# Folding the even frequencies of the first transform a third time, with part of the fold on GpSimd

## The chip, the cores and the metric

The kernel runs on one core of one Trainium2 chip. The metric is the device time of one execution in microseconds. A core has five engines that run side by side, each through its own instructions in a fixed order, and wait for one another through semaphores: PE (TensorE) multiplies matrices, DVE (VectorE) and ACT (ScalarE) work element by element, POOL (GpSimd) does so too and issues transfers, SP (SyncE) here only issues transfers. PEld is PE's loading of weights, which runs beside its matmuls.

## The reference

```python
def _attn_ref(x):                       # x: (8, 1856, 256) float32
    X = np.fft.fft(x, axis=1)
    X = np.fft.fft(X, axis=2)
    return X.real.astype(np.float32)

def _moe_ref(x, w_group, w_expert, w1, w2):   # x: (14848, 256)
    g_idx = np.argmax(x @ w_group, axis=1)    # 4 groups; g_w = its softmax weight
    ...
    for g in range(4):
        e_idx = np.argmax(x[g_idx == g] @ w_expert[g], axis=1)   # 4 experts per group; e_w
        for e in range(4):
            h = np.maximum(xg[mask_e] @ w1[g, e], 0.0)           # 256 -> 1024
            ye = h @ w2[g, e]                                    # 1024 -> 256
            out[tok_idx] = combined[:, None] * ye                # combined = g_w * e_w
```

The real part of a two-dimensional Fourier transform of each of 8 batches of 1856 x 256 gives 14848 tokens; each goes to one of 16 experts (256 to 1024 to 256), and the result is scaled by the two softmax weights.

## The kernel before

**The first transform.** It runs over the 1856 positions of a batch, as matrix multiplication with cosine and sine tables (`CS`, resident in on-chip memory). Symmetry cuts the work before that. The host lays out x in four quarters (`_layout`): positions s, 928 - s, -s and 928 + s, for s = 0 to 464, in 4 chunks of 128 rows, the mirrored two with their columns reversed. `fold` (one generator per batch) adds these quarters: `fold_rows` adds the two halves of x on DVE for batches 0 and 1; for later batches the second half is added by the transfer itself (`load_x`: one plain load on SP's queue, then two accumulating loads that POOL issues). `squares` and `total` give the sum of squares for a power-of-two scale. `quarters(pm)` adds (pm = 0) or subtracts (pm = 1) the remaining two halves, two DVE instructions of 128x514 each, from `xa` into `xc` (both tiles named `xq`). `columns(eo, ...)` folds the 256 columns (eo = 0 adds, 1 subtracts) into `BD[:, pm, eo]`, 512 columns wide: 4 chunks of 128. `hi_half` (ACT) scales to float16 as the high half of `ghl`, `lo_half` (DVE) makes the rest, the low half.

`s_stage` multiplies: for odd frequencies (par = 1, 464 of them) and even ones (par = 0, 465), and for cosine (tr = 0) and sine (tr = 1, 127 weight columns), 12 matmuls add up in a bank `pu`: 4 chunks of positions times three products of high and low halves. `sums` lists them. For par = 1 the products with the high half come first. Then the sum is split into float16 halves `U` (`split_later`: ACT copies it, PE subtracts it, ACT copies the rest). The same sums for the Nyquist column of all batches run once, with 8 weight columns (`xngh`, `nyquist_in`, `nyquist`); their result goes through memory (`UND`, `UN`, then row 127 of `U` for each batch, scaled in `un`).

**After it.** `d_stage` is the second transform, over features, of the batch before (`pr`, with the router's logits into `look`); `route` finds the experts and each token's place (DVE mostly), `leftovers` lets POOL copy odd tiles into `Um`, `lookup` turns places into gather indices (`ii_e`). The expert stage (`phase2`, lines 1296 to 1317: `ph`, `py`) gathers rows with indirect transfers (`xg`), transposes them (`xT`) and begins while the last batch is still being routed.

**What sets the order.** All steps of the first stage are generators, and the tables `START` and `ORDER0` to `ORDER8` at the top of the file are the order in which they are advanced, one letter a step: S is `s_stage`, D `d_stage`, R `route`, T and Z `lookup` and the rest of an older route, F and N the folds of the next and the next but one batch, L, U, W, X leftovers, Nyquist rows, first weights and first gathered rows; G and H the fold of batch 0 and the Nyquist preparation; small letters release queued copies (l: low halves, s, I, i: splits, d: rows). Each engine then keeps the order in which instructions were written (`InOrder`), so a step that waits holds back all that stands behind it on its engine. The line 281 in the profile is the call in `InOrder` through which all of these are recorded, so tiles tell them apart.

Buffers: `xq` has four halves, two per batch, so batch b + 2 is loaded into those of batch b; `BD` has one buffer, `ghl` two, `pu` four banks, `pr` two.

Of the kernel before, what the change touches and what calls it, by code (L numbers as in the profile page):

```python
# [57 lines left out]
START = 'iTGHDiHFGGGtHGI'  # L58
ORDER0 = 'WSDDGYZSlZZZFFWRiSdSDFdIDLilFisiFZsTItFFldtUIdLRSiFtilFilSdI'
ORDER1 = 'ZZsLDbldDsDDlDIIdDdRSFblLDFSULdStFiFFFlRIRRFStRiRSRRRtNRUZDRNRURbTlITLdRtNTNSRNslsTUILIFsStTRtTsSRTRiSTSSI'  # L60
ORDER2 = 'ldslZZFZUDZLLRDtlIDDddSZDTFRiZlsssRsDbIZbLsSSFDLRiiRFSsDRRlRNTRURtISdRDTNRNTIdRRtdSFRdsSZNTFiTTbNtRTRUSUsTSSSIN'
ORDER3 = 'IZDslILiFZDIlLZLdFUZZRTFlUDSFdSSLFSLSSDItFTFRRDSIFURLDRRsRTDFRNRTSSFLsiRTDISITTURRsSNRNRUNTITRRRNR'
ORDER4 = 'bstZTDDDZdDbLIDlDLULDFlDSLslZDItiDRbdFRRSUDlIZFFTstSisDLIRNSSINDUsRdNINtsRbFiTRRISRDTSSNRRTTRDiTTlRU'
ORDER5 = 'DUslITSIFdFbLRIIZSRDLRdsZSZlIbZNIFRSsZRFDSsdRRSdUDlINLRRDUsLlTNRFlDRSIsssdtSTNFUITNFUlbRiUZdTUDRTsZT'
ORDER6 = 'DTSSFLdstRtsIFtZZlIRLdSZRZsILIUUIRZNLFRNSSLRNLDdLRUDLRZlNDbNNTiNsSFtLsLlDLITSTDsTNdNNisRUlLsTFiZRdNR'
ORDER7 = 'IZNWSSZZtLNLdFdiFDLFiDsFdWUDTdZZZSUDDdlsdtlDdLIRDRRdRRDWRWtRSRSSsiXUiRINRRLtZslTRDSXIIiWXlRbTStRXXRtsUWXWiXlTtXLSWWUllSRbRXWIWWWTTXbilWSWWWTWbWWWWTsW'
ORDER8 = 'IDsiDdDLdRbLLddDRdLsLRiDdRDR|RDDLLbidbTsiRTRRRRRTRLdisbLRRld|R|RRRRDRLRRLRRRR'
# [5 lines left out]
CW = 4 * NK  # L73
# [229 lines left out]
class K:  # L303
# [82 lines left out]
    def nyquist_in(self):  # L386
# [29 lines left out]
        V.tensor_tensor(out=gv, in0=gv, in1=bc(sn[:, :], 1, 8), op=ALU.mult)  # L416
        yield
# [59 lines left out]
    def fold(self, b, x, fp):  # L477
# [58 lines left out]
        if b == 0:  # L536
# [4 lines left out]
            quarters(0)  # L541
            columns(0, 0, 1)
# [406 lines left out]
    def phase1(self):  # L949
# [4 lines left out]
        with tc.tile_pool(name="ua", bufs=1) as ua, tc.tile_pool(name="fft", bufs=1) as fp:  # L954
# [616 lines left out]
```

## Time and profile before

| what | value |
|---|---|
| time, median of 3 runs | 895.41 us (891.83 to 895.62) |
| the profiled execution | 892.05 us, span 890.2 us |
| PE busy | 823.2 us, 92% (6491 matmuls) |
| DVE / ACT / POOL busy | 546.6 / 577.0 / 313.5 us |
| first matmul of the expert stage | at 193.5 us |
| first transform's matmuls | 384, with 83.8 us busy |

The span runs from the first to the last instruction. A busy PE is not PE at its peak: matmuls follow each other before the former has ended, so the spacing of their starts says more than their length. The same holds for DVE, whose instructions overlap by some 0.08 us. An engine's share over the whole span mixes stages; the rows below are therefore mostly of stretches.

### The profile page before, as it was taken

The page shows a single profiled execution, that of the slowest core. Times are in us where ns is not written, and L with a number is a line of the kernel's source. Part 1 is how long each engine was busy: PE and PEld are TensorE (multiplying, and loading weights), DVE is VectorE, ACT ScalarE, POOL GpSimd, SP SyncE. Part 2 cuts the span into 40 slices and gives each one's busy share as a digit, 9 for nine tenths or more (in the row PEclk, how much of TensorE's full clock was granted, in tenths as well). Part 3 has the DMA queues.
Part 4 walks back from the last instruction along what each step waited for, and adds up shares of the span by engine and source line. Part 5 has one row for each costly group of instructions (what it writes and reads, how often), then busy time and mean ns, then how long its engine had stood idle before and what let it go on. Part 6 is the DMA issues. An engine that isn't in the chain of part 4 may idle for free.

```text
span 890.2 us, 17777 instructions
## 1 busy us (share of the span) xinstructions
PE 823.2 (92%) x6491; PEld 587.2 (66%) x6491; DVE 546.6 (61%) x1381; ACT 577.0 (65%) x1190; POOL 313.5 (35%) x326
## 2 busy tenths in 40 slices
PE   2799999889697999999999999999999999999996
PEld 0367666556455767776767676767676768686865
DVE  6479998579574656464747474747474756564440
ACT  2477676576633877586858585858686777775541
POOL 1032211412674524434343434344343435240303
PEclk9999999899999999999999999999999999999999
DMA  9677863364667355555646454646555746443201
GB/s 351 176 226 201 243 210 121 137 210 138 186 180 197 111 189 181 158 155 166 173 156 178 149 166 155 173 160 172 161 176 152 196 147 206 127 137 66 55 10 41
DMA packets 105515, 144.53 MB, mean 162 GB/s; under 512 B 75194, under 2 KB 77638, under 8 KB 103888
## 3 DMA queue, kind: packets, MB, share of 16 engines
q1 hardware_dynamic: 91360, 106.15, 39.4%
q0 software_dynamic: 13632, 36.99, 14.5%
q8 instruction: 52, 0.85, 0.4%
q10 hardware_dynamic: 432, 0.22, 0.1%
q14 instruction: 39, 0.32, 0.1%
HBM read 97.41 MB, written 31.72 MB: 145 GB/s over the span
## 4 chain that ended last, share of the span: by engine, by line
PE 58%; DVE 11%; issue 8%; ACT 5%; DMA 5%; POOL 2%; another core or an unknown queue 2%; SPq 1%; POOLq 0%; DVEq 0%; ACTq 0%
PE ph L1296 29%; PE py L1312 24%; DMA xT<-xh 3%; PE pu L281 2%; ACT whl L281 2%; POOL out L940 2%; PE pr L281 1%; DVE whl L281 1%; DMA wst<-w 1%; DVE xq L281 1%; ACT junk L281 1%; SPq L1266 1%; DVE ghl L281 1%; DVE xT L281 1%
## 5 line engine op out<-in xcount | busy, mean ns | idle before, releaser
L1312 PE MATMUL py<-whl,hT 128*128 128x256 f16 x2976 | 357.4, 273 | 13.6 <-ACT y L1317 9.8
L1296 PE MATMUL ph<-xT,whl 128*128 128x512 f16 (+2 forms) x2112 | 358.4, 318 | 10.6 <-DMA xT<-xh 4.8
L1312 PEld LDWEIGHTS <-hT 128*128 128x128 f16 x2976 | 289.2, 98 | 71.4 <-issue 15.2
L1300 DVE SCALAR_TENSOR_TENSOR hT<-ph,hT 128x512 f16<-128x512 f32 (+2 forms) x352 | 179.7, 529 | 194.1 <-ACT hT L1299 126.6
L1296 PEld LDWEIGHTS <-whl 128*128 128x128 f16 x2112 | 182.5, 98 | 134.1 <-issue 16.6
L940 POOL DMA_INDIRECT out<-y,tok x124 | 147.3, 1188 | 332.2 <-ACT y L1317 266.2
L1299 ACT ACTIVATE hT<-ph 128x512 f16<-128x512 f32 (+2 forms) x352 | 157.2, 473 | 116.0 <-PE ph L1296 68.1
L281 DVE SCALAR_TENSOR_TENSOR whl<-wst,e_v,whl 128x1024 f16<-128x1024 f32 x112 | 138.0, 1279 | 20.1 <-ACT whl L281 18.0
L1238 POOL DMA_INDIRECT xg<-XS,ii_s x100 | 105.5, 1055 | 86.7 <-ACT xh L1258 35.7
L281 ACT ACTIVATE whl<-wst,e_v 128x1024 f16<-128x1024 f32 x112 | 121.0, 1138 | 15.2 <-DVE e_v L281 11.4
L281 ACT ACTIVATE junk<-wst 128x1024 bf16<-128x1024 f32 x112 | 119.2, 1064 | 6.0 <-DMA wst<-w 5.1
L1317 ACT ACTIVATE y<-py,cws 128x256 f32<-128x256 f32 x124 | 57.2, 471 | 52.0 <-PE py L1312 41.2
L281 PE MATMUL pu<-CS,ghl 128*128 128x464 f16 (+3 forms) x384 | 83.8, 370 | 3.5 <-ACT ghl L281 3.5
L1260 DVE TENSOR_TENSOR xh<-xg,xh 128x256 f16<-128x256 f32 x112 | 46.3, 418 | 48.7 <-ACT xh L1258 35.7
L1258 ACT CAST xh<-xg 128x256 f16<-128x256 f32 x112 | 42.4, 402 | 38.6 <-DMA xT<-xh 34.7
L281 PEld LDWEIGHTS <-ghl 128*128 128x128 f16 (+1 forms) x384 | 44.5, 120 | 33.2 <-issue 3.6
L281 PEld LDWEIGHTS <-U 128*128 128x128 f16 x672 | 44.9, 100 | 19.2 <-issue 7.0
L281 PE MATMUL pr<-c,U 128*128 128x256 f16 x336 | 49.9, 286 | 4.9 <-DMA U<-un 2.5
L281 ACT CAST U<-pu 128x464 f16<-128x464 f32 (+3 forms) x64 | 32.8, 548 | 20.0 <-PE pu L281 19.0
L281 POOL DMA_DIRECT2D xq<-xq x12 | 11.0, 1072 | 88.5 <-ACT xT L281 27.1
L281 DVE TENSOR_TENSOR xq<-xq 128x514 f32<-128x514 f32 x40 | 25.4, 688 | 6.4 <-DMA xq<-xq 6.2
L281 ACT ACTIVATION_READ_ACCUMULATOR junk<-wst 128x1 f32 x112 | 23.2, 207 | 0.0
(184 smaller groups left out, 461.1 us busy)
## 6 DMA issues: line engine op xcount, KB each, us to landing
wst<-w SPq DMA_DIRECT2D x108, 512.0 KB
xq<-xq SPq DMA_DIRECT2D x8, 1028.0 KB
xq<-xq POOLq DMA_DIRECT2D x12, 514.0 KB
XS<-whl SPq DMA_DIRECT2D x6, 910.0 KB
CS<-cs SPq DMA_DIRECT2D x8, 464.5 KB
XS<-row SPq DMA_DIRECT2D x3, 1040.0 KB
XS<-row SPq DMA_DIRECT2D x3, 910.0 KB
XS<-xq SPq DMA_DIRECT2D x3, 910.0 KB
```

Of the source, the lines that this page charges most:

```text
L281: return self.tc.keep_in_program_order(f(*args, **kw))
L940: ins = self.nc.gpsimd.indirect_dma_start(out=out, out_offset=bass.IndirectOffsetOnAxis(ap=ap, axis=0), in_=in_, in_offset=None, bounds_ch ...
L1238: ins = self.nc.gpsimd.indirect_dma_start(out=xg[:, :].bitcast(I32), out_offset=None, in_=self.XS[:, :], in_offset=bass.IndirectOffsetOnAx ...
L1258: A.copy(xh[:, 0], xg[:, 0:D])
L1260: lo = V.tensor_tensor(out=xh[:, 1], in0=xg[:, 0:D], in1=xh[:, 0], op=ALU.subtract)
L1266: Q.dma_start(out=xT[:, :, j * P:(j + 1) * P], in_=xh, transpose=True)
L1296: nc.tensor.matmul(ph[:, 0:n * P], lhsT=w[:, wl, o:o + P], rhs=xT[:, xl * 2 + c, :], start=i == 0, stop=i == 5)
L1299: nc.scalar.activation(hT[:, f, 0], ph[:, 0:n * P], AF.Relu)
L1300: nc.vector.scalar_tensor_tensor(out=hT[:, f, 1], in0=ph[:, 0:n * P], scalar=0.0, in1=hT[:, f, 0], op0=ALU.max, op1=ALU.subtract)
L1312: nc.tensor.matmul(py, lhsT=hT[:, f, hl, j * P:(j + 1) * P], rhs=w[:, wl, 2048 + f * D:2048 + (f + 1) * D], start=i == 0, stop=i == 23)
L1317: nc.scalar.activation(y, py, AF.Copy, scale=cw)
```

## The change

A third fold: for even frequencies position 464 - s has the same cosine as s or its negative, so that half of the positions are enough once sums and differences are formed. The table's even columns split into those that are 2 (232 of them) and 0 (233) modulo 4, each with 2 chunks of positions in place of 4; the host places the positions above 232 in the last two chunks in reverse (`_place`), the table shrinks from 4 x 929 to 4 x 464 + 2 x 465 columns per trigonometric function and half, and is loaded in 6 pieces in place of 8. On the chip the even column passes write to the scratch `tw` (which lies in `xa`), and `again` makes their sum and difference into `BD`, in two instructions. From batch 2 on, `quarters(0)` is done by GpSimd. For batch 0 the odd half is now folded first. The Nyquist preparation gets three small instructions. All order tables are new.

```diff
@@ -23,6 +23,7 @@
 P = 128
 KO, KE = 464, 465
 NK = KO + KE
+KH = 232
 NU = 936
 UJ, UN = 16, 117
 NT = 7
@@ -55,22 +56,22 @@
 
 
 
-START = 'iTGHDiHFGGGtHGI'
...
-ORDER2 = 'ldslZZFZUDZLLRDtlIDDddSZDTFRiZlsssRsDbIZbLsSSFDLRiiRFSsDRRlRNTRURtISdRDTNRNTIdRRtdSFRdsSZNTFiTTbNtRTRUSUsTSSSIN'
...
+START = 'llSZFGSHRHHGGGilHZsUGTL'
...
+ORDER2 = 'ZIZZtiFdFiDDFRUSDLZdTTDDtbZFsZLsssRSFNFLSTdSRSTLZsStNFSRRRTLIFRdDDRRTIUITiLRTsURTTSNsRTDTNRDNTRRRRsbIU'
...
 ORDERS = (ORDER0, ORDER1, ORDER2, ORDER3, ORDER4, ORDER5, ORDER6, ORDER7)
 WAIT = 4
 SUMS = 2
 BIG = 1.0e6
 RS = 2.0 ** -11
-CW = 4 * NK
+CW = 4 * KO + 2 * KE
 E23 = 2.0 ** 23
 
 
@@ -136,20 +137,26 @@
 
 
 def _kcols():
-    ev = np.arange(2, 928, 2)
-    n = NT * P - KO
-    return np.concatenate([np.arange(1, 929, 2), ev[:n], ev[n:], [0, 928]])
+    return np.concatenate([np.arange(1, 929, 2), np.arange(2, 928, 4), np.arange(4, 928, 4), [0, 928]])
+
+
+def _place(s):
+
+    return np.where(s <= KH, s, 256 + KO - s)
 
 
 def _constants():
-    s = np.arange(512)
+    s = np.arange(465)
     k = _kcols()
     ang = 2 * np.pi * ((s[:, None] * k[None, :]) % S) / S
-    ok = (s <= 464)[:, None]
-    cs = np.zeros((P, 2, 2, 4, NK), np.float16)
+    cs = np.zeros((P, 2, 2, CW), np.float16)
     for tr, fn in enumerate((np.cos, np.sin)):
-        for hl, m in enumerate(_hilo(np.where(ok, fn(ang), 0.0))):
-            cs[:, tr, hl] = m.reshape(4, P, NK).transpose(1, 0, 2)
+        for hl, m in enumerate(_hilo(fn(ang))):
+            odd, even = np.zeros((512, KO)), np.zeros((256, KE))
+            odd[_place(s)] = m[:, :KO]
+            even[:KH + 1] = m[:KH + 1, KO:]
+            cs[:, tr, hl, :4 * KO] = odd.reshape(4, P, KO).transpose(1, 0, 2).reshape(P, -1)
+            cs[:, tr, hl, 4 * KO:] = even.reshape(2, P, KE).transpose(1, 0, 2).reshape(P, -1)
 
     l = _features()
 
@@ -230,10 +237,11 @@
     xq = np.zeros((B, 4, 512, 257), x.dtype)
     for q in range(4):
         u = s[use[q]]
+        to = _place(u)
         if q < 2:
-            xq[:, q, u, :256] = x[:, idx[q, u], :]
+            xq[:, q, to, :256] = x[:, idx[q, u], :]
         else:
-            xq[:, q, u, 1:] = x[:, idx[q, u], ::-1]
+            xq[:, q, to, 1:] = x[:, idx[q, u], ::-1]
     xn = np.ascontiguousarray(
         xq[:, :, :, 128].reshape(B, 4, 4, P).transpose(3, 1, 2, 0)).reshape(P, -1)
     xq = np.ascontiguousarray(
@@ -414,6 +422,10 @@
         V.tensor_tensor(out=g[:, 1], in0=t[:, 0], in1=t[:, 1], op=ALU.subtract)
         gv = g.rearrange("p a (c b) -> p (a c) b", b=B)
         V.tensor_tensor(out=gv, in0=gv, in1=bc(sn[:, :], 1, 8), op=ALU.mult)
+        a, z = g[:, 0, 0:2 * B], g[:, 0, 2 * B:4 * B]
+        V.tensor_copy(out=t[:, 0, 0:2 * B], in_=a)
+        V.tensor_tensor(out=a, in0=a, in1=z, op=ALU.add)
+        V.tensor_tensor(out=z, in0=t[:, 0, 0:2 * B], in1=z, op=ALU.subtract)
         yield
         gh = self.fp.tile([P, 2, 2, 4, B], F16, name="xngh")
         ghv = gh.rearrange("p h a c b -> p h (a c b)")
@@ -453,8 +465,11 @@
 
     def sums(self, par, tr, terms):
 
-        k0, n = ((KO, KE), (0, KO))[par]
-        return [(0, n, c, cl, gl, c * NK + k0) for c in range(4) for (gl, cl) in terms]
+        if par:
+            return [(0, KO, c, cl, gl, c * KO) for c in range(4) for (gl, cl) in terms]
+        at = 4 * KO
+        return [(o, w, c + 2 * (i if tr else 1 - i), cl, gl, at + c * KE + o)
+                for i, (o, w) in enumerate(((0, KH), (KH, KE - KH))) for c in range(2) for (gl, cl) in terms]
 
     def load_x(self, b, xp, parts=1):
 
@@ -502,14 +517,23 @@
 
         def quarters(pm):
             for h in (0, 2):
-                V.tensor_tensor(out=xc[:, 4 * pm + h:4 * pm + h + 2], in0=xa[:, h:h + 2],
+                (self.G if b >= SUMS and pm == 0 else V).tensor_tensor(out=xc[:, 4 * pm + h:4 * pm + h + 2], in0=xa[:, h:h + 2],
                                 in1=xa[:, 4 + h:6 + h], op=(ALU.add, ALU.subtract)[pm])
 
-        def columns(eo, m0, m1):
-            t = xc[:, 4 * m0:4 * m1].rearrange("p (m c) d -> p m c d", c=4)
-            V.tensor_tensor(out=BD[:, m0:m1, eo].rearrange("p m (c d) -> p m c d", d=128),
-                            in0=t[:, :, :, eo:eo + 128], in1=t[:, :, :, 256 - eo:128 - eo:-1],
+        tw = xa.rearrange("p a d -> p (a d)")[:, 0:1024].rearrange("p (m n) -> p m n", m=2)
+
+        def columns(eo, m):
+            t = xc[:, 4 * m:4 * m + 4]
+            out = tw[:, m] if m == eo else BD[:, m, eo]
+            V.tensor_tensor(out=out.rearrange("p (c d) -> p c d", d=128),
+                            in0=t[:, :, eo:eo + 128], in1=t[:, :, 256 - eo:128 - eo:-1],
                             op=(ALU.add, ALU.subtract)[eo])
+
+        def again(m0, m1):
+            o = BD.rearrange("p m e n -> p (m e) n")[:, 3 * m0:3 * m1 - 2:3]
+            for i in range(2):
+                V.tensor_tensor(out=o[:, :, 256 * i:256 * i + 256], in0=tw[:, m0:m1, 0:256],
+                                in1=tw[:, m0:m1, 256:512], op=(ALU.add, ALU.subtract)[i])
 
         def lo_half(part):
             V.scalar_tensor_tensor(out=part(hl[:, 1]), in0=part(BD), scalar=sx, in1=part(hl[:, 0]),
@@ -538,18 +562,21 @@
             hl = fp.tile([P, 2, 2, 2, 512], F16, name="ghl", bufs=2)
             self.fds[b] = hl, v
             total()
-            quarters(0)
-            columns(0, 0, 1)
+            quarters(1)
+            columns(0, 1)
             V.tensor_scalar(out=ei, in0=pn.bitcast(I32), scalar1=24, scalar2=None,
                             op0=ALU.logical_shift_right)
             V.tensor_scalar(out=sx.bitcast(I32), in0=ei, scalar1=-E23, scalar2=199 * E23, op0=ALU.mult,
                             op1=ALU.add)
+            hi_half(lambda t: t[:, 1, 0])
+            quarters(0)
+            columns(0, 0)
+            again(0, 1)
             hi_half(lambda t: t[:, 0, 0])
-            quarters(1)
-            columns(0, 1, 2)
-            hi_half(lambda t: t[:, 1, 0])
-            yield
-            columns(1, 0, 2)
+            yield
+            columns(1, 0)
+            columns(1, 1)
+            again(1, 2)
             lo_half(lambda t: t[:, :, 0])
             yield
             hi_half(lambda t: t[:, :, 1])
@@ -569,9 +596,11 @@
         hl = fp.tile([P, 2, 2, 2, 512], F16, name="ghl", bufs=2)
         self.fds[b] = hl, v
         for eo in range(2):
-            for m in range(2):
-                columns(eo, m, m + 1)
-            yield
+            for m in (eo, 1 - eo):
+                columns(eo, m)
+            yield
+        again(0, 2)
+        yield
         exponent()
         yield
         exponents()
@@ -963,10 +992,11 @@
             self.load_small()
             xs = {0: self.load_x(0, xp, 2)}
             self.CS = fp.tile([P, 2, 2, CW], F16, name="CS")
-            cs = self.ap["cs"].rearrange("p (t h c k) -> p t h c k", t=2, h=2, c=4)
+            cs = self.ap["cs"].rearrange("p (t h k) -> p t h k", t=2, h=2)
+            cut = (0, 2 * KO, 4 * KO, CW)
             for tr in range(2):
-                for c in range(4):
-                    nc.sync.dma_start(out=self.CS[:, tr, :, c * NK:c * NK + NK], in_=cs[:, tr, :, c])
+                for a, z in zip(cut, cut[1:]):
+                    nc.sync.dma_start(out=self.CS[:, tr, :, a:z], in_=cs[:, tr, :, a:z])
                 if tr == 0:
                     nc.sync.dma_start(out=self.c16, in_=self.ap["c16"])
                     xs[1] = self.load_x(1, xp)
```

DVE at the start, from before batch 0's second fold to its first low halves; `xq` are the quarters (and, 512 wide, the scratch), `BD` the folded columns, `xng` the Nyquist column. Before:

```order
L281 TENSOR_TENSOR xq<-xq 128x514 x4
L281 TENSOR_TENSOR BD<-xq 128x512
L281 TENSOR_SCALAR x_ei<-misc 128x1
L281 TENSOR_SCALAR x_v<-x_ei 128x1
L281 TENSOR_TENSOR xq<-xq 128x514 x2
L281 TENSOR_TENSOR BD<-xq 128x512
L281 TENSOR_TENSOR BD<-xq 128x2x512
L281 SCALAR_TENSOR_TENSOR ghl<-BD,x_v,ghl 128x2x512
L281 TENSOR_TENSOR xnt<-xn 128x64
L281 TENSOR_TENSOR xng<-xnt 128x32 x2
L281 TENSOR_TENSOR xng<-xng,n_v_189 128x64
```

and now:

```order
L289 TENSOR_TENSOR xng<-xng 128x16
L289 TENSOR_TENSOR xng<-xnt,xng 128x16
L289 TENSOR_TENSOR xq<-xq 128x514 x4
L289 TENSOR_TENSOR BD<-xq 128x512
L289 TENSOR_SCALAR x_ei<-misc 128x1
L289 TENSOR_SCALAR x_v<-x_ei 128x1
L289 TENSOR_TENSOR xq<-xq 128x514 x2
L289 TENSOR_TENSOR xq<-xq 128x512
L289 TENSOR_TENSOR BD<-xq 128x256 x2
L289 TENSOR_TENSOR BD<-xq 128x512
L289 TENSOR_TENSOR xq<-xq 128x512
L289 TENSOR_TENSOR BD<-xq 128x256 x2
```

The Nyquist steps now stand ahead of the second fold (four more of them above these rows), and the low halves (`ghl`), which come next, have three column passes and four half passes ahead of them after the scale `x_v`.

POOL, from the accumulating loads of batch 3 on; the numbers tell buffers apart (now `xq_238` and `xq_391` are batches 2 and 3, `xq_644` batch 4; `U_243` is batch 0). Before:

```order
L281 DMA xq_386<-xq 128x1028 x2
L281 COPY Um_384<-U_234 128x2x33
L281 ISA
L281 TENSOR_SCALAR Um_384<-U_234 128x2x33
L281 COPY Um_384<-U_234 128x2x31
L281 TENSOR_SCALAR Um_384<-U_234,c32_78 128x2x31
L281 DMA xq_641<-xq 128x1028 x2
```

and now:

```order
L289 DMA xq_391<-xq 128x1028 x2
L289 COPY Um_381<-U_243 128x2x33
L289 ISA
L289 TENSOR_SCALAR Um_381<-U_243 128x2x33
L289 COPY Um_381<-U_243 128x2x31
L289 TENSOR_SCALAR Um_381<-U_243,c32_78 128x2x31
L289 TENSOR_TENSOR xq_239<-xq_238 128x514 x2
L289 TENSOR_TENSOR xq_392<-xq_391 128x514 x2
L289 DMA xq_644<-xq 128x1028 x2
```

The additions of batches 2 and 3 stand together between batch 0's leftovers and batch 4's accumulating loads.

DVE after batch 1's low halves; `mx`, `dd`, `m`, `oh` and `pe` are batch 0's route. Before:

```order
L281 SCALAR_TENSOR_TENSOR ghl<-BD,x_v,ghl 128x512 x4
L281 TENSOR_TENSOR xq<-xq 128x514 x4
L281 TENSOR_TENSOR BD<-xq 128x512 x2
L281 TENSOR_REDUCE mx<-lg 128x14
L281 TENSOR_TENSOR dd<-lg,mx 128x14x4
L281 SCALAR_TENSOR_TENSOR m_550<-dd,c_78 128x56
```

and now:

```order
L289 SCALAR_TENSOR_TENSOR ghl<-BD,x_v,ghl 128x512 x4
L289 TENSOR_SCALAR un<-UN,x_v 128x117
L289 TENSOR_REDUCE mx<-lg 128x14
L289 TENSOR_TENSOR dd<-lg,mx 128x14x4
L289 TENSOR_TENSOR xq<-xq 128x514 x2
L289 SCALAR_TENSOR_TENSOR m_544<-dd,c_78 128x56
```

Batch 2's quarters and first column passes stood before the route's first instruction; now two of the four quarters stand behind it and the column passes further on.

## Rows read from the trace of the kernel before

**Rows 1.** The chain that ended last: its shares of the span by engine and line
```profile
PE ph L1296 29%; PE py L1312 24%; DMA xT<-xh 3%; PE pu L281 2%; ACT whl L281 2%; POOL out L940 2%; PE pr L281 1%; DVE whl L281 1%; DMA wst<-w 1%; DVE xq L281 1%; ACT junk L281 1%; SPq L1266 1%; DVE ghl L281 1%; DVE xT L281 1%
```

**Rows 2.** Busy time by stretch; columns as the first line names them
```profile
core 0: us, PE busy (x) PEld busy (x) DVE busy (x) ACT busy (x) POOL busy (x), PEclk, DMA share, GB/s
44.00:157.50 113.50, 109.00 (x962) 77.17 (x963) 98.45 (x273) 79.31 (x178) 24.41 (x41) 0.98 0.67 197
62.00:116.40 54.40, 53.47 (x482) 37.99 (x481) 51.61 (x141) 40.76 (x91) 15.36 (x22) 1.00 0.80 235
157.50:194.00 36.50, 29.28 (x235) 19.86 (x234) 24.93 (x73) 23.35 (x57) 13.56 (x21) 0.86 0.46 149
```

**Rows 3.** The chain in order of time, 75 to 125 us: start, us, what
```profile
83.35 2.58 DVE BD L281 x4
...
105.26 2.50 DVE BD L281 x4
```

**Rows 4.** What DVE waited for, 44 to 157.5 us: total, times, longest
```profile
DVE mx L281 <- ACT lg L281: 5.3, 3, 3.4
DVE ghl L281 <- ACT ghl L281: 2.1, 1, 2.1
DVE base L281 <- PE look L281: 2.0, 1, 2.0
```

**Rows 5.** PE in order of time: start, us, engine, line, operation, tiles, shape, count
```profile
83.61 0.82 PE L281 MATMUL pr<-c,U 128*128 128x256 f16 x6
84.27 0.31 PE L281 MATMUL look<-RW,U 128*128 128x40 f16 x6
...
87.65 9.61 PE L281 MATMUL pu<-CS,ghl 128*128 128x464 f16 x48
```

**Rows 6.** Weight loads by form, 0 to 200 us: busy us, mean ns, idle
```profile
L281 PEld LDWEIGHTS <-ghl 128*127 128x127 f16 x192 | 26.1, 139 | 11.4 <-issue 0.6
```

**Rows 7.** DVE passes by form, 0 to 200 us: busy us, mean ns, idle
```profile
L281 DVE TENSOR_TENSOR BD<-xq 128x512 f32<-128x512 f32 x30 | 19.1, 688 | 0.2
```

**Rows 8.** POOL: forms (busy, mean), `Um` durations (min/median/max), a row by time
```profile
L988 POOL MEMSET xg<- 128x260 f32 x8 | 2.1, 304 | 0.0
...
L818 POOL MEMSET xq<- 128x16 f32 x4 | 0.4, 107 | 0.1
...
L281 POOL COPY Um<-U x16: 224/243/1098, 50.1 to 189.0; 128x66 f16<-128x66 f16 x8, 128x62 f16<-128x62 f16 x8
L281 POOL TENSOR_SCALAR Um<-U x8: 391/526/831, 50.4 to 188.5; 128x66 f16<-128x66 f16 x8
...
84.76 1.40 POOL L281 TENSOR_SCALAR Um<-U,c 128x62 f16<-128x62 f16 x1
```

**Rows 9.** All engines in order of time at the start, in brackets the wait before
```profile
16.71 2.50 PE L281 MATMUL pu<-CS,ghl 128*128 128x464 f16 x6 [3.46 <-ACT ghl L281]
...
16.95 1.28 DVE L281 SCALAR_TENSOR_TENSOR ghl<-BD,x_v,ghl 128x1024 f16<-128x1024 f32 x1
...
34.68 0.36 SPq L281 DMA_DIRECT2D UND<-xT  x1
...
41.77 0.26 DVE L281 TENSOR_SCALAR un<-UN,x_v 128x117 f16<-128x117 f16 x1 [5.70 <-DMA UN<-UND]
...
43.98 0.60 PE L281 MATMUL pr<-c,U 128*128 128x256 f16 x3 [2.55 <-DMA U<-un]
```

**Rows 10.** The same at the stage's end
```profile
158.24 1.69 POOL L1238 DMA_INDIRECT xg<-XS,ii_e  x1 [12.39 <-DVE ghl L281]
...
168.10 1.08 POOL L1238 DMA_INDIRECT xg<-XS,ii_e  x1 [0.30 <-issue]
...
172.97 5.90 PE L281 MATMUL pu<-CS,ghl 128*127 128x464 f16 x18
...
179.35 0.41 ACT L281 CAST xh<-xg 128x256 f16<-128x256 f32 x1
...
193.52 2.32 PE L1296 MATMUL ph<-xT,whl 128*128 128x512 f16 x10
```

More of the change, by code (lines that the diff above doesn't have):

```diff
@@ L51 @@
 RATE, RATE2, T1, T2 = 1000, 800, 320, 2570
-START = 'iTGHDiHFGGGtHGI'
-ORDER0 = 'WSDDGYZSlZZZFFWRiSdSDFdIDLilFisiFZsTItFFldtUIdLRSiFtilFilSdI'
-ORDER1 = 'ZZsLDbldDsDDlDIIdDdRSFblLDFSULdStFiFFFlRIRRFStRiRSRRRtNRUZDRNRURbTlITLdRtNTNSRNslsTUILIFsStTRtTsSRTRiSTSSI'
-ORDER2 = 'ldslZZFZUDZLLRDtlIDDddSZDTFRiZlsssRsDbIZbLsSSFDLRiiRFSsDRRlRNTRURtISdRDTNRNTIdRRtdSFRdsSZNTFiTTbNtRTRUSUsTSSSIN'
[L62 to L67, printed above, removed]
+START = 'llSZFGSHRHHGGGilHZsUGTL'
+ORDER0 = 'ilFSGSZdtbZtYZdDFblFDStIilFlTsRiFWtFSTDWlFtDDZTtILLdiULZdSiSZdSiFIlZlFbFF'
+ORDER1 = 'LTibDtZDdULlZLZdtbbZDiRsSFdFILUtDFFItSRRlFdRSiSRlSRRFFRlILRNRNiURlbTNlUsSslIISFRIdNTFtNtRstiRSZDRTdITtUUSbT'
+ORDER2 = 'ZIZZtiFdFiDDFRUSDLZdTTDDtbZFsZLsssRSFNFLSTdSRSTLZsStNFSRRRTLIFRdDDRRTIUITiLRTsURTTSNsRTDTNRDNTRRRRsbIU'
+ORDER3 = 'bDdZLlZDZbLItUlIDDbiRDdDdSbFTFDSiDSRFDZtsiFDLRisdLISRtSFIUIUNFDlSRSTlbTsRRTRiRSNNlRsDSLlTsRDIsTTTNNRTRUZRRb'
+ORDER4 = 'LbbDdZlstZtDULIlIDZbRStDdiFDSDsDSTDFZFIFLLiDsRdIRUStRFISNiiRTSRFTDSINRRTSNTllsRbSRTsRDTTUDNRTRsRNIbR'
+ORDER5 = 'ZTRFsUidFtDDRllILZSRFSdsZiSUDFRLNUlDlIRSNIdlNsSSsslRDdlStNNlRRFFRDTSRtLDdTUZlSRTUIRRTDiZT'
+ORDER6 = 'DTSsLtRZiSLdtSssTFFRLDZIZINISdURNsDNltNRNddNsiRdLbZNZRSSRIRbDTDLdLFidbUNsRRlNiZILNLdiZTNTdLDTIdRUZFUIRTRsSts'
+ORDER7 = 'ZlDSNddNdIlZdLSFWiDDZTFdSZZtsUDdWdlDZlUdDRtRRWIRDSRDbZLLRINIRsiRWRtRSXSbRRIsDiXDNiTtSUZlTWIXRlSRSsXWXitRXXbSXWWUTTUdRSILRllXWWWSWSbUWTbWWtTWWIWsWSWTWssW'
+ORDER8 = 'iIRDLDDIsdLLDRdLT|dLbDiDddDiRLRIRsRLIdTRDlsRiblbbdRRlRTLTsI|dRLRLIDRRRRRblRRR|RDddRRRsRL'
 ORDERS = (ORDER0, ORDER1, ORDER2, ORDER3, ORDER4, ORDER5, ORDER6, ORDER7)
```

## The prediction

> **What bounds the kernel now.** I began with the chain that ended last, by engine and line [rows 1]: 53% of the span is the expert stage (`ph`, `py`), which the change does not touch; the first transform's matmuls (`pu`, with two other kinds) have 2%, and DVE's lines 1% each. So the change can only move the first stage, up to about 194 us, and what hangs on its end. The stretches [rows 2] show that stage. From 44 to 157.5 us PE is busy 109.00 of 113.50 us and DVE 98.45; between 62 and 116.4 us they have 53.47 and 51.61 of 54.40, so both are full at once. There the chain runs along DVE [rows 3], piece after piece with little between. DVE's waits in the whole stretch [rows 4] are short and few; 9.4 us of them (5.3 + 2.1 + 2.0) are for what PE and ACT deliver. [...]
>
> **PE's part of the change.** Each batch has 48 matmuls of 464 or 465 columns against the table, 24 for odd and 24 for even frequencies. The 24 even ones become 24 of 232 or 233; their count, their weight loads and the splitting of the sums stay. In [rows 5] 48 of the long ones take 9.61 us; without the 0.36 that the last of them takes alone, 47 follow each other at 0.197 us. Six of 256 columns take 84.27 - 83.61 = 0.66 us, 0.110 each. Between the two a column costs (0.197 - 0.110)/208 = 0.00042 us, so 232 columns take 0.100. Saved per batch: 24 x 0.097 = 2.3 us; over 8 batches 18.6, and 1.2 more in the Nyquist sums (12 even ones halved).
>
> Half of the shortened matmuls have 127 weight columns, and such a load lasts 139 ns [rows 6]. Under a 464-column matmul it was hidden; if it were not under 0.100 us, those 96 would be spaced 0.139 and 96 x 0.039 = 3.7 us would go back. I take 0.100, since a load runs beside the matmul ahead of it, and keep the 3.7 for the range.
>
> **DVE's part.** From batch 2 on, two 128x514 passes (`quarters(0)`) leave DVE and two 128x512 passes (`again`) come; both kinds follow each other at 0.60 us (four `BD` in 2.50, the last 0.69 long) [rows 3, 7]. Net: nothing. Before that DVE gains work only: batch 1 two passes of 0.6 us, which fit into its 5.70 us wait for the Nyquist rows [rows 9] and cost nothing while that wait stands (1.2 if it goes); batch 0 four of 256 columns, 1.4 us (0.34 each, an estimate: half of 0.60 and a little for the start of each); three small Nyquist steps, 0.6 (0.2 each, by the 0.26 us of the 117-element `un` in [rows 9]). As the transforms of the middle of the stage cannot come faster than DVE makes `ghl`, PE's 6 x 2.3 = 14 us (batches 1 to 6) turn into time only as far as DVE's waits for PE and ACT shrink: at most 9.4, of which I take 9.
>
> **GpSimd's part.** 12 passes of 128x514, two inputs, now run on POOL. No such row exists before. Bounds from the nearest rows [rows 8]: the 128x260 MEMSET follows at 0.26 us (eight in 2.1), so 514 elements take at least 0.5 us; the fastest `Um` multiply of 66 elements takes 391 ns, less the 107 ns of the smallest POOL row 284, and 514/66 of that is 2.2, so about 2.3 us. Nearest is the plain `Um` copy, 224 ns at best: 0.107 + 0.117 x 7.8 = 1.0. With a second input I take 1.3.
>
> They don't run beside DVE freely. In [rows 8] the multiply of 66 elements takes 0.39 us at best; one of 62 takes 1.40 us while DVE runs `BD` passes (83.35 to 85.93 us, [rows 3]); the median of the copies is near the minimum, the maximum five times it. POOL waits for DVE there; so short are its instructions that DVE loses nothing one can see (four `BD` in 2.58 instead of 2.50). A POOL instruction of 1.3 us can turn that round. Price for DVE per pass: 0 if the wait is POOL's alone, the full 1.3 if DVE's next two-input instruction always stands behind it. I take half, 0.65, on the ten passes of batches 3 to 7: 6.5 us (batch 2's passes fall into the stretch where DVE waits for `lg`, 3.4 us at longest [rows 4]). With the bounds of the duration it is 0 to 23. [...]
>
> Who waits for POOL: `columns(0, 0)`, the first even pass on DVE, and behind it the whole row of DVE. In the second order excerpt the batch-2 and batch-3 passes stand behind batch 0's four `Um` instructions and ahead of batch 4's accumulating loads. The first of the four began at 50.1 us before [rows 8]; with 1.3 for the four and two passes of 1.3, batch 2's even columns can't start until about 54, while before DVE folded them ahead of the route. PE has room for that: DVE's `ghl` passes run ahead of the sums that read them. Scratch in `xa` keeps that buffer until `again`, so batch 4's load may start later once: 0 to 3 us, taken as nothing, since it is used a batch period later.
>
> **Start.** The Nyquist steps (four and the new three, 7 x 0.2 = 1.4 us) move ahead of batch 0's second fold, but the odd half's first pass is now ready after one column pass instead of two, sooner by two quarters and a column pass of 0.6 each. First matmul: 16.71 + 1.4 - 1.8 = 16.3 [rows 9]. The low halves come later: they began at 16.95 [rows 9], and now have the 1.4 and four half passes (1.4) more ahead of them, so 19.7, and end 1.28 later. PE stops after its eight high matmuls; the halved Nyquist sums, 1.2 us shorter, win part of it back. What releases PE at 43.98 is a chain of three DMAs from 34.68 on, 9.3 us long and unchanged [rows 9]. The last Nyquist copy before it moves by about a microsecond: **-1** (-3 to +1).
>
> **End.** Batch 7's sums ran slowly, 18 matmuls in 5.90 us, 0.33 each against 0.20 [rows 10, 5], after PE had stood; its `ACT xh` waited in order behind the copies of those sums until 179.35, though the gathers had been issued from 158.24 on. Halved even sums bring these copies earlier: at least 2.3 us, at most the 10 or so between the last gather's issue (169.2) and 179.35. **-5** (-1 to -10).
>
> **Sum**, against the profiled execution's own 892.05 us (span 890.2): -1 - 9 + 6.5 - 5 = -8.5, so 883.5. The median of the runs, 895.41, lies 3.4 above that execution; on its scale **887**. After 194 us nothing is touched, and I expect the shift to pass through.
>
> **Rivals.** [...] (C) *DVE pays in full*: 10 x 1.3 = 13, -2 in all, 893; no change. For it: DVE is 95% busy from 62 to 116.4 us [rows 2], so there is nearly always a two-input pass next. [...] (D) *GpSimd becomes the bound of the fold*: a pass takes the upper 2.3 us, `columns(0, 0)` waits for two of them behind loads and `Um`, batch after batch: 10 x 2.3 = 23 against the 15 gained, +8, 903; with some of it hidden, +5. It decides from 1.5 us per pass on, if DVE loses all of it. Against: the plain copy's rate. (E) *PE's saving doesn't appear* because the 127-column loads show: +3.7, of which DVE's cap hides most; it lies inside (C).
>
> **Chances.** Forecast 0.48 (its own range 882 to 891), B 0.20, C with E 0.20, D 0.12. A measurement of this kernel tells about 0.5%, 4.5 us, from no change: faster means below 890.9, slower above 899.9. Forecast and B are faster (0.68), C is the same (0.20), D slower (0.12). The range takes in B and C and the lower part of D: 874 to 898; above it remains about 0.1, below it some 0.05.
>
> **What would show it.** Right: `pu` matmuls of 232 columns spaced 0.10 us with either weight width; DVE's idle time between 44 us and the end of the last `ghl` below 8 us; POOL's 128x514 passes 1 to 2 us long, with gaps in DVE's row beside them; the first `ph` 6 to 12 us earlier than 193.5. Wrong: a spacing near 0.14 on 127-column weights; DVE stopping at `columns(0, 0)` for POOL (D); no gaps on DVE beside POOL's passes (B); the first `ph` moved but the end not, which would put a wait of the expert stage's start (weights, gathers) in place of the first transform.

## The result and the profile after

The changed kernel is about 1% slower: 902.86 us (median of 5; 901.82 to 907.62) against 895.41 (891.83 to 896.77), ratio 1.0105 with a 95% interval of 1.0069 to 1.0140. A second comparison, on the chip of the last group below, gave 1.0125 (1.0084 to 1.0166). The forecast was 887. The profiled execution is the longest of the five (907.62, span 905.8); what follows therefore rests on the stretch up to the first expert matmul, and is compared with the second trace of either kernel.

PE's busy time in the same three stretches as [rows 2] of the kernel after:

```profile
44.00:157.50 113.50, 93.98 (x879) 71.24 (x878) 99.69 (x242) 71.44 (x161) 39.48 (x53) 0.91 0.66 192
62.00:116.40 54.40, 46.01 (x452) 35.02 (x453) 51.57 (x129) 35.74 (x80) 21.76 (x28) 0.97 0.78 227
157.50:194.00 36.50, 27.58 (x223) 19.86 (x221) 25.87 (x80) 24.60 (x60) 10.10 (x16) 0.89 0.29 95
```

PE fell from 53.47 to 46.01 us of the 54.40 between 62 and 116.4 us; DVE, with fewer instructions (129 for 141), stayed as full as it was. The work has not become less for the engine that was full; it has become longer per instruction. The chain by line says the same: `BD` and `xq`, the fold, have 5% where the row of before [rows 1] gave `xq` 1% and had no `BD`.

```profile
PE ph L1326 27%; PE py L1342 24%; DMA xT<-xh 4%; PE pr L289 4%; DVE xq L289 3%; ACT whl L289 2%; PE pu L289 2%; DVE BD L289 2%; DMA wst<-w 1%; ACT junk L289 1%; POOL out L969 1%; DVE xT L289 1%; DVE ghl L289 1%; PE look L289 1%; ACT hT L1329 1%
```

Where DVE's time went shows when GpSimd's rows are laid beside DVE's. GpSimd's passes (durations min/median/max in ns, then three pairs by time: start, us):

```profile
L289 POOL TENSOR_TENSOR xq<-xq x12: 1259/1356/1824, 49.4 to 139.9; 128x514 f32<-128x514 f32 x12
...
49.42 2.49 POOL L289 TENSOR_TENSOR xq<-xq 128x514 f32<-128x514 f32 x2
54.71 3.12 POOL L289 TENSOR_TENSOR xq<-xq 128x514 f32<-128x514 f32 x2 [2.79 <-DMA xq<-xq]
...
114.52 2.75 POOL L289 TENSOR_TENSOR xq<-xq 128x514 f32<-128x514 f32 x2 [5.44 <-DMA xq<-xq]
```

DVE in order of time in the same moments:

```profile
50.26 1.73 DVE L289 TENSOR_TENSOR dd<-lg,mx 128x56 f32<-128x56 f32 x1
...
54.93 1.77 DVE L289 TENSOR_TENSOR BD<-xq 128x512 f32<-128x512 f32 x1
56.62 1.76 DVE L289 TENSOR_TENSOR xq<-xq 128x512 f32<-128x512 f32 x1
...
59.94 1.28 DVE L289 TENSOR_TENSOR BD<-xq 128x512 f32<-128x512 f32 x2
...
114.89 0.20 DVE L289 TENSOR_REDUCE mx<-lg 128x15 f32<-128x60 f32 x1
115.12 0.98 DVE L289 TENSOR_TENSOR dd<-lg,mx 128x60 f32<-128x60 f32 x1
116.03 1.29 DVE L289 TENSOR_SCALAR un<-UN,x_v 128x117 f16<-128x117 f16 x1
```

`dd` on 56 columns lasts 1.73 us and ends at 51.99, when GpSimd's pair ends (51.91); undisturbed it lasts 0.22, and `un` 0.25:

```profile
59.56 0.22 DVE L289 TENSOR_TENSOR dd<-es,mx 128x56 f32<-128x56 f32 x1
...
43.26 0.25 DVE L289 TENSOR_SCALAR un<-UN,x_v 128x117 f16<-128x117 f16 x1
```

`BD` and `xq` passes last 1.77 and 1.76 beside a pass, and 1.28 for two of them when GpSimd is still. The instruction held can be tiny: `dd` ended with the second of GpSimd's two passes and `un` with its pair (117.32 and 117.27 us), while `BD` ended at 56.70, 0.55 us after the first pass (56.15); what each lost was the rest of a pass, or of both, not a share of its own length. Such a hold counts as busy and as no wait, so the list of waits does not have it. DVE's waits in 44 to 157.5 us, after, beside [rows 4] (total, times, longest):

```profile
DVE mx L289 <- ACT lg L289: 7.4, 3, 6.5
DVE off L289 <- PE misc L289: 2.9, 2, 1.8
DVE ghl L289 <- ACT ghl L289: 1.3, 1, 1.3
```

No wait is for POOL. The wait of `mx` for `lg` grew from 3.4 (4.4 in g1) to 6.5 at its longest, because the six passes of batch 2 that DVE had done ahead of it now stand behind it (four) or had gone to GpSimd (two).

PE in order of time (in brackets the wait before):

```profile
125.58 0.56 PE L289 MATMUL misc<-oh,c 128*128 128x240 f16 x2 [3.13 <-DVE oh L289]
...
127.36 1.49 PE L289 MATMUL pr<-c,U 128*128 128x256 f16 x6
...
131.80 0.82 PE L289 MATMUL pr<-c,U 128*128 128x256 f16 x6
...
140.46 2.56 PE L289 MATMUL pu<-CS,ghl 128*128 128x232 f16 x24
```

The last row holds all 24 shortened matmuls of a batch, 12 of them with 127 weight columns, though it names only the first's width. They follow each other at 2.56/24 = 0.107 us, or 0.100 without the 0.26 that the last takes alone; the last 11 of them, all with 127 weight columns, take 1.26 us, 0.100 again. After PE has stood for DVE (3.13 us), six `pr` take 1.49 us instead of 0.82: the granted clock was 0.50 from 127.3 to 131.6 us and 1.00 from 131.7 to 135.0. The granted clock of 0.91 in the middle, 0.98 before, is the mean over such stretches. Whether it is the loss or only goes with it, e4 was made to tell.

One account serves for all runs: from the first scaling of the Nyquist rows (the first `un` on DVE) to the first expert matmul (`ph`). Columns: stretch, its length, DVE busy (instructions), clock, DMA share, GB/s. Before, after, e1 and e2:

```profile
41.77:193.52 151.75, 125.13 (x345) 0.96 0.61 183
```

```profile
39.69:200.62 160.93, 135.82 (x343) 0.89 0.57 170
```

```profile
39.01:193.43 154.42, 130.99 (x353) 0.92 0.58 175
```

```profile
39.89:212.24 172.35, 147.24 (x341) 0.87 0.52 157
```

The table has the same for the runs spoken of here; "not busy" is length less busy. The groups e, f and g ran on one chip each, with their own runs of the kernel before (medians 893.05, 883.98 and 895.50 us). Traces of the kernel before are from the first comparison and from group g alone, so the times of e and f in the table are laid beside those of other chips; group f's ran the kernel before some 10 us faster. The ratios leave out one execution of e2 (1695 us) and one of e3 (3013 us), far slower than all others.

| kernel | ratio to before (95%) | first `un` | first `ph` | DVE busy | not busy |
|---|---|---|---|---|---|
| before | 1 | 41.77 | 193.52 | 125.13 | 26.62 |
| after | 1.0105 (1.0069 to 1.0140) | 39.69 | 200.62 | 135.82 | 25.11 |
| e1 all on DVE | 0.9998 (0.9974 to 1.0022) | 39.01 | 193.43 | 130.99 | 23.43 |
| e2 GpSimd twice | 1.0237 (1.0205 to 1.0269) | 39.89 | 212.24 | 147.24 | 25.11 |
| e3 before + GpSimd | 1.0082 (1.0052 to 1.0112) | 41.37 | 201.01 | 127.42 | 32.22 |
| e4 even sums twice | 1.0144 (1.0105 to 1.0182) | 39.08 | 198.38 | 133.20 | 26.10 |
| f1 third fold, old order tables | 1.0061 (1.0037 to 1.0085) | 38.64 | 193.23 | 130.22 | 24.37 |
| f2 third fold in 0, 1, 7 | 1.0027 (1.0003 to 1.0051) | 41.42 | 191.58 | 125.24 | 24.92 |
| f3 DVE twice | 1.0073 (1.0045 to 1.0101) | 40.24 | 198.82 | 139.04 | 19.54 |
| f4 pieces | 1.0113 (1.0076 to 1.0150) | 38.91 | 195.11 | 135.52 | 20.68 |
| g1 before again | 1.0000 (0.9974 to 1.0026) | 41.65 | 192.47 | 124.62 | 26.20 |
| g2 after again | 1.0125 (1.0084 to 1.0166) | 38.90 | 199.27 | 136.19 | 24.18 |
| g3 old order tables, 0 and 7 | 0.9996 (0.9970 to 1.0022) | 41.77 | 191.00 | 125.20 | 24.03 |
| g4 old order tables, 0, 1, 7 | 1.0009 (0.9981 to 1.0037) | 42.01 | 192.69 | 125.04 | 25.64 |

### The profile page after: what moved, and what is told of

Read it like the earlier page. It is cut to its first block, busy times and chain, and to the rows that moved or that the text cites. A ratio compares the mean times of both kernels' runs of the same rounds, so it can differ in the third digit from the quotient of the medians.

```text
span 905.8 us, 17798 instructions
## 1 busy us (share of the span) xinstructions
PE 817.2 (90%) x6491; PEld 590.5 (65%) x6491; DVE 560.7 (62%) x1391; ACT 577.1 (64%) x1190; POOL 322.9 (36%) x338
## 4 chain that ended last, share of the span: by engine, by line
PE 59%; DVE 14%; issue 9%; ACT 8%; DMA 7%; POOL 1%; another core or an unknown queue 1%; SPq 1%; POOLq 0%; ACTq 0%; DVEq 0%
PE ph L1326 27%; PE py L1342 24%; DMA xT<-xh 4%; PE pr L289 4%; DVE xq L289 3%; ACT whl L289 2%; PE pu L289 2%; DVE BD L289 2%; DMA wst<-w 1%; ACT junk L289 1%; POOL out L969 1%; DVE xT L289 1%; DVE ghl L289 1%; PE look L289 1%; ACT hT L1329 1%
## 5 line engine op out<-in xcount | busy, mean ns | idle before, releaser
L969 POOL DMA_INDIRECT out<-y,tok x124 | 143.6, 1158 | 329.9 <-ACT y L1347 293.0
L289 PE MATMUL pu<-CS,ghl 128*128 128x464 f16 (+5 forms) x384 | 67.6, 331 | 3.9 <-DVE ghl L289 2.0
L289 PEld LDWEIGHTS <-U 128*128 128x128 f16 x672 | 47.7, 104 | 22.6 <-issue 7.1
L289 PE MATMUL pr<-c,U 128*128 128x256 f16 x336 | 54.5, 304 | 5.9 <-DMA U<-un 2.0
L289 DVE TENSOR_TENSOR xq<-xq 128x514 f32<-128x514 f32 (+1 forms) x44 | 31.0, 737 | 5.9 <-DMA xq<-xq 5.8
L289 POOL TENSOR_TENSOR xq<-xq 128x514 f32<-128x514 f32 x12 | 17.4, 1464 | 29.1 <-DMA xq<-xq 21.4
```

The costliest lines, as they stand in the source:

```text
L289: return self.tc.keep_in_program_order(f(*args, **kw))
L969: ins = self.nc.gpsimd.indirect_dma_start(out=out, out_offset=bass.IndirectOffsetOnAxis(ap=ap, axis=0), in_=in_, in_offset=None, bounds_ch ...
```

## The experiments

Theory H: each GpSimd pass holds DVE, which bounds the middle of the stage. Rivals: the emptier PE at a lower clock makes the loss (K), the waits that the new order tables bring make it (O), PE's time and not DVE's is what counts in the middle (P).

**e1, the additions back on DVE.**

```diff
-                (self.G if b >= SUMS and pm == 0 else V).tensor_tensor(out=xc[:, 4 * pm + h:...
+                V.tensor_tensor(out=xc[:, 4 * pm + h:...
```

> The changed kernel with the additions of quarters(0) for batches 2 to 7 back on DVE, at the same steps and with the same tables. Theory H (each GpSimd pass holds one DVE instruction for about 1.05 us, and DVE is the bound of the middle of the stage): DVE loses 12 x 0.6 = 7.2 us and gets back 12 x 1.05 = 12.6, so 5.4 us faster than the changed kernel, about 897.5, and no DVE TENSOR_TENSOR of 128x512 above 0.75 us. Rival K (PE, emptier, falls to the lower clock, and that is the loss): the passes' hold costs nothing, DVE is 7 us fuller, about 903 to 910 and the granted clock as low as before. Rival O (the new tables make the waits): 903 to 910 too, the wait of mx for lg stays at 6.5 us.

Measured: 0.9998, that is 9.6 us below the changed kernel (11.3 by its second comparison), where H had 5.4; the first `ph` is 7.2 us earlier. DVE has 12 passes more and is busy 4.83 us less. With 12 x 0.6 = 7.2 for these passes, GpSimd's had cost DVE 4.83 + 7.2 = 12.0 us, 1.0 a pass. Counted another way, by how much longer each form of DVE instruction is on the mean than in e1 (`dd<-lg,mx` on 56 columns: 593 ns for 214), the holds are 11.1 us in the first trace of the changed kernel and 12.6 in the second (g2). K and O fall as the cause: the clock is still 0.92 in this stretch, the order tables are the same, and the loss is gone.

**e2, GpSimd's passes done twice.**

```diff
-            for h in (0, 2):
-                (self.G if b >= SUMS and pm == 0 else V).tensor_tensor(out=xc[:, 4 * pm + h:4 * pm + h + 2], in0=xa[:, h:h + 2],
+            gp = b >= SUMS and pm == 0
+            for h in (0, 2, 0, 2) if gp else (0, 2):
+                (self.G if gp else V).tensor_tensor(out=xc[:, 4 * pm + h:4 * pm + h + 2], in0=xa[:, h:h + 2],
```

> The changed kernel with each of the 12 GpSimd passes done twice in a row (the second writes the same values again). Theory H: 12 more holds of about 1.05 us on the bound, +12.6 us, about 915. Rivals K and O: only what waits for the second pass is later, 0 to 3 us, about 903 to 906.

Measured: 1.0237, against 1.0105 for 12 passes; DVE is busy 11.4 us more than after, 0.95 a pass (form by form against e1: 23.0 for its 24 passes), its time not busy is the same, and the first `ph` is 11.6 us later. GpSimd and DVE at batch 2:

```profile
49.62 4.96 POOL L289 TENSOR_TENSOR xq<-xq 128x514 f32<-128x514 f32 x4
```

```profile
50.54 4.13 DVE L289 TENSOR_TENSOR dd<-lg,mx 128x56 f32<-128x56 f32 x1
```

A DVE instruction of 0.22 us stands for 4.13, to the end of the last of four passes (54.58): four in a row didn't let it in between.

**e3, the kernel before with the additions on GpSimd, and nothing else.** The line is that of e1's minus, put into the old kernel.

> The kernel before with one thing changed: quarters(0) of batches 2 to 7 on GpSimd, old tables, no third fold. Theory H: DVE gains 7.2 us and loses 12.6, +5.4 us against the kernel before, about 901. Rivals K and O, by which the hold costs nothing: DVE gains 7.2 us where it is the bound, about 888 to 891. If GpSimd's passes come late behind its loads (the prediction's rival D), more than 901.

Measured: 1.0082, about 7 us slower: this one part alone makes a loss of nearly the same size, but only in part by the holds. DVE has 7.2 us less to do and is busy 2.3 more: 9.5 us of holds. Of the 7.9 us by which the stretch is longer, the holds less the work that left are thus 2.3; the other 5.6 is time not busy, most of it from a wait that the changed kernel's own order avoided (it takes in the 3.4 us that DVE waited for `lg` there before):

```profile
51.04 2.50 POOL L281 TENSOR_TENSOR xq<-xq 128x514 f32<-128x514 f32 x2
```

```profile
53.57 1.29 DVE L281 TENSOR_TENSOR BD<-xq 128x512 f32<-128x512 f32 x2 [8.10 <-POOL xq L281]
```

In the old order batch 2's column passes stand ahead of the route, and wait 8.10 us for GpSimd, which comes to the additions after `Um` (rival D's mechanism, once).

**e4, the shortened sums made twice** (24 matmuls more a batch), so that PE has as many columns as before again.

```diff
+            if par == 0:
+                for i, (o, w, c, cl, gl, at) in enumerate(terms):
+                    self.M.matmul(pu[0:m, o:o + w], lhsT=hl[:, gl, pm, tr, c * 128:c * 128 + m],
+                    ...
             for i, (o, w, c, cl, gl, at) in enumerate(terms):
```

> The changed kernel with the shortened even sums made twice (the second pass starts the bank anew, so the values are the same): PE has its old 2.6 us a batch back. Theory H: PE is not the bound in the middle, 0 to +3 us (batch 7's sums at the end), 903 to 906. Rival K: a fuller PE keeps the higher clock, 3 to 6 us faster, about 898. The prediction's own assumption (PE's time turns into time): 8 x 2.6 = +20, up to 920.

Measured: 1.0144 (1.0105 to 1.0182), which overlaps the intervals of both comparisons of the changed kernel (1.0105, 1.0125). The row of the stretches, 44 to 157.5 us:

```profile
44.00:157.50 113.50, 101.69 (x1023) 81.20 (x1021) 99.22 (x244) 71.63 (x164) 40.91 (x53) 0.97 0.65 189
```

PE is busy 7.7 us more there and its clock is back at 0.97 (0.91 after, 0.98 before), and nothing is won: the lower clock goes with the loss and doesn't make it. Some 8 x 24 x 0.107 = 20 us of matmuls cost 1.7 or 3.5 us by the medians (with both intervals, from -3 to 8), and the first `ph` comes no later. In this kernel, with GpSimd's holds in it, PE's time is nearly free in the middle, so saving it is worth nearly nothing.

**f1, the third fold alone, old order tables**: e1's line, the order tables of before, and the third fold's two passes in the step of the last column passes.

> The third fold alone: all passes on DVE, the old order tables (the third fold's two passes in the step of the last column passes). Theory H (DVE bounds the middle): DVE has 1.2 us more for each of batches 2 to 7, +7.2, the start gives -2 and the end -3.5, so 0 to +3 against the kernel before. Rival P (PE's 2.3 us a batch turn into time): -6 to -15.

Measured: 1.0061, +5 us, somewhat above H's range; DVE busy 130.22, as in e1. By itself the third fold gains nothing (e1) or loses (f1, whose order tables were not made for it); P's gain isn't there.

**f2, the third fold in batches 0, 1 and 7 alone** (new order tables, all passes on DVE; the cosine and sine table `CS` has four chunks again for the even frequencies):

```diff
-            out = tw[:, m] if m == eo else BD[:, m, eo]
+            out = tw[:, m] if m == eo and b in THIRD else BD[:, m, eo]
```

> All passes on DVE, the changed kernel's tables, the third fold only in batches 0, 1 and 7; batches 2 to 6 have four chunks of positions (even matmuls of 465 columns) as before. Theory H: DVE's middle is 5 x 1.2 = 6 us lighter than in e1 and PE has its old load there, where both were nearly full; start and end keep what they gained: 5 to 6 us faster than the kernel before, about 888 on this scale of 893. Rival P: PE is the bound again in the middle, so no faster than e1 (0).

Measured: 1.0027, no gain; H's 5 to 6 us were missed, and no faster than e1 is what P had. In the stretch H's count does show: DVE is busy 5.75 us less than in e1, and the stretch is 4.3 shorter. But the first `un` came at 41.42, not at 39.0 to 39.7, so the start's gain was not there, and of the 4.3 us 1.9 are left at the first `ph`. Why the whole has not even these stays open; that PE, which has its old work back in five batches, has a part in it is not excluded. The start's gain was there in all runs with the smaller `CS` (38.6 to 40.2) and in none with the larger one (f2, g3 and g4: 41.4 to 42.0; e3: 41.37; before: 41.65 and 41.77). That the loading of `CS` makes it was not tried by itself.

**f3, the additions twice on DVE**: e2's line with `V`.

> As e1 (all passes on DVE), but quarters(0) of batches 2 to 7 done twice in a row on DVE. Theory H: 12 passes of 0.6 us on the bound, +7.2 us against e1, against +11.8 that the same repetition cost on GpSimd in e2. Rival P: DVE has room while PE is the bound, 0 to +2.

Measured: 1.0073 against e1's 0.9998, so some 6.6 us for 12 passes (with both intervals, 3 to 10). In the traces DVE is busy 8.05 us more and the stretch is 4.2 longer, since 3.9 of it went into time not busy (`mx`'s waits for `lg` fell from 6.3 to 3.1). So DVE's work was worth between half and all of itself: half here, three quarters in f2, all in e2. A repeated pass cost DVE 0.95 us when it ran on GpSimd (e2), 0.67 when it ran on DVE itself.

**f4, GpSimd's passes in halves**:

```diff
-            for h in (0, 2):
...
+            gp = b >= SUMS and pm == 0
+            n = 1 if gp else 2
+            for h in range(0, 4, n):
...
```

> The changed kernel with each GpSimd pass cut in two (24 of 128x257 in place of 12 of 128x514). If a pass holds DVE for its own length: 24 x 0.55 us, the same time as the changed kernel (+7.5 against before). If each instruction costs DVE a fixed microsecond: +12 more. If DVE gets its turn between two pieces and goes on beside the second: less, down to +2.

Measured: 1.0113, the same as whole passes. GpSimd, then DVE beside the second four:

```profile
L289 POOL TENSOR_TENSOR xq<-xq x24: 717/728/1191, 48.8 to 138.5; 128x257 f32<-128x257 f32 x24
...
54.37 4.29 POOL L289 TENSOR_TENSOR xq<-xq 128x257 f32<-128x257 f32 x4 [2.81 <-DMA xq<-xq]
```

```profile
54.58 1.22 DVE L289 TENSOR_TENSOR BD<-xq 128x512 f32<-128x512 f32 x1
55.72 1.21 DVE L289 TENSOR_TENSOR xq<-xq 128x512 f32<-128x512 f32 x1
56.86 1.21 DVE L289 TENSOR_TENSOR BD<-xq 128x512 f32<-128x512 f32 x1
```

Three DVE passes lose 0.55 each where two lost 1.09: here the hold went with GpSimd's time, not with the number of its instructions (DVE busy 135.52 us, 135.82 after), and cutting didn't help. The trace's first `ph`, 195.11, is 5.5 us before that of the changed kernel, by 4.4 us less time not busy; the whole gained nothing, and where f4 loses it stays open without a trace of the kernel before on that chip.

**g1 and g2, the two kernels once more, g3 and g4, the third fold in batches 0 and 7, or 0, 1 and 7, with the old order tables.**

> The kernel before once more, for a trace on the same chip as the others of this call: ratio 1.00, first expert matmul at 193 to 194 us as in the first trace. If the first matmul or the rest behind it differ by several us from the first trace, that is the spread between runs, and single traces say nothing on the expert stage below that.

> The changed kernel once more: +7 to +8 us against before, first expert matmul 7 us later than that of before. If the part after the first expert matmul is again 8 us longer than that of before, the tables cost time there too; if it is equal, the 8 us of the first trace were that run's.

> All passes on DVE, old tables, the third fold in batches 0 and 7 alone. Theory H: DVE in the middle has its old work, batch 7 1.2 us more; the start gives 2 us, batch 7's shorter sums 1 to 3: 2 to 4 us faster than before. Rival (the end is bound by ACT, the gathers and DVE there, not by batch 7's sums): the start's 2 us less 1.2, no difference.

> As g3, and batch 1 too: DVE 1.2 us more beside its wait for the Nyquist rows, PE 2.3 less between 44 and 62 us. Theory H: the same as g3 within 1 us. Against f2 (same work, new tables): if f2's lack of gain was the tables', 2 to 4 us faster than f2.

Measured: 1.0000, 1.0125, 0.9996 and 1.0009. g1 and g2 repeat the account: first `ph` 6.8 us later, DVE busy 11.6 more. g3's first `ph`, 191.00, is 1.5 us before g1's, and the whole is the same, as the rival of its expectation had it; but the 2 us of the start, on which both theories counted, did not come (first `un` 41.77), and the interval is some 2 us wide to either side, so which is right isn't shown. g4 is 1.6 us below f2 by the ratios, inside the noise: that f2's missing gain was its order tables' isn't shown either. No version tried is faster than the kernel before. Behind the first `ph` (span less its start) the traces have 696.7 and 697.8 us for before, 705.2 and 704.2 for after, but 702.8 for e1 and 704.7 for g4, which took the same time as before in their medians (the traces of after, e1 and g4 lie 4 to 5 us above their medians). So part of the changed kernel's loss, 0 to 4 us by the medians, may lie there; single traces don't settle it, and it stays open.

## Why the prediction was wrong

By its own steps, at the first `ph` (forecast 185, 8.5 earlier; measured 200.62, 7.1 later):

- *PE's part* was right: 0.100 to 0.107 us for 232 columns (0.100 said), and the matmuls with 127 weight columns follow each other at the same 0.100. Rival E is out.
- *The start*, -1: right in direction, -2.1 at the first `un`, but in part by luck: what it was worked out from, the Nyquist steps' new place and their halved sums, is in f2 too, whose first `un` came at 41.42.
- *The duration of a GpSimd pass*, 1.3 us: right, median 1.36.
- *The price of a pass to DVE failed.* "I take half, 0.65, on the ten passes of batches 3 to 7: 6.5 us." Measured 12.0 on all 12 (e1; 11.1 and 12.6 counted form by form), 0.95 more for each further one (e2). The half was a middle between two bounds with no row behind it, and batch 2's passes were taken as free in DVE's wait for `lg`. They stood behind `Um` and came when that wait was over (49.42), and the route's first instruction was held. Rival C had nearly this price in sum (13, as 1.3 on ten passes; measured 1.0 on twelve); B, that GpSimd gives way and DVE loses nothing, is out.
- *DVE's waits failed more*: "at most 9.4, of which I take 9", with another -5 for the end. The two can be told apart at the start of the last 30 of batch 7's table matmuls, 172.97 us before [rows 10] and 182.45 after (row below). From the first `un` to there DVE's time not busy was 23.34 us before and 23.10 after: of the 9 nothing came, 0.2 (1.2 between the second traces, g1 and g2). From there to the first `ph` it took 20.55 before and 18.17 after, so of the 5 for the end 2.4 came, inside its bounds (-1 to -10). The waits of [rows 4] were not waits for the sums that became shorter: by their tiles `mx` and `base` wait for the second transform and the router (`lg`, `look`), whose work is unchanged, and `ghl` for ACT's high half. Before the longest, PE ran nothing but `pr` and `look` from 43.98 to 50.83 us; for the others it is argued. That PE and DVE were both full [rows 2] was read as two bounds that share the gain; e4 and e2 show the one: 20 us more on PE did not make the first `ph` later, 11.4 us more on DVE moved it by 11.6.
- *DVE's net work*: "nothing"; in this stretch 7.2 left and 5.9 came (e1 less before), so -1.3. (This and the holds are one count: with 11.1 for the holds it is -0.4.)

The row of after at which the middle and the end are told apart:

```profile
182.45 4.44 PE L289 MATMUL pu<-CS,ghl 128*127 128x464 f16 x18
```

Together: -2.1 (start) - 1.3 (net work) + 12.0 (holds) - 1.5 (DVE's time not busy, middle and end: 26.62 to 25.11) = +7.1; or, by place, -2.1 (start) + 11.6 (middle) - 2.4 (end). Against the forecast's terms, the holds were taken 5.5 too small, and the gain of waits and end 12.5 too large, nearly 9 of it in the middle's waits; the second alone makes the forecast of a gain wrong. Rival C had the right mechanism and the wrong time, 893, because it kept the -15 (-1 - 9 - 5). Rival D had nearly the time (903) by luck, for another reason: DVE never waited for a GpSimd result in the changed kernel, only in e3. Against the half stand the rows of after: a DVE instruction stood until GpSimd's passes ended (`dd` 1.73 us for 0.22, ending at 51.99 behind their 51.91; `un` 1.29 for 0.25). Not every instruction did: beside a pass `mx` took 0.20 us, as elsewhere.

## What to carry to other kernels

Work moved from a full DVE to GpSimd is not taken off DVE when GpSimd's instructions hold DVE's: here a 0.60 us pass became one of 1.36 us that cost DVE 1.0. Look for it as DVE instructions of unlike lengths in one form (here `dd` on 56 columns with 0.22 and 1.73 us), since it counts as busy and stands in no list of waits. Before a saving on one of two full engines is counted, ask of each wait on the other whether it ends on the very work that is saved; doubling that work, as in e4, tells in one run what it is worth in that kernel.

## What the runs showed of the hardware

- GpSimd's two-input addition held DVE instructions with two inputs (`dd` 1.73 us for 0.22, `BD` 1.77 for 0.68), and `un`, a float16 instruction with one (1.29 for 0.25); `TENSOR_REDUCE` (`mx<-lg`) took 0.20 us beside it and 0.20 to 0.21 elsewhere.
- GpSimd's passes in a row left DVE no gap in one place (`dd` 4.13 us through four in e2), and took turns with it in another (1.77 and 1.76 us, with a pass each). In both DVE's instruction had begun while a pass was running (at 50.54 us behind 49.62 in e2, at 54.93 behind 54.71 after); why it came in between two passes in the one place alone is not shown. In the second GpSimd's pair took longer too, 3.12 us instead of 2.49, its second pass 1.72 instead of 1.26.
